# Value sums written straight into a value buffer, a fourth buffer for exponentials, and a new instruction order

## The chip, the cores and the metric

One Trainium2 chip, one of its cores. The metric is the device time of one execution, in microseconds (us). A kernel is run several times and the median is given beside the lowest and the highest. The profile comes from one further execution, in which every instruction's start and duration are recorded; its span is the time from the first to the last instruction, and a little more than the span passes before and after it.

## The reference

Two stages. The first is attention over 4 batches, 8 heads, 768 positions and 64 channels a head. Each position attends to its neighbours within a window of 16 and to 24 summaries, one for each block of 32 positions (the maximum of the block's keys, the mean of its values):

```
k_sum = k.reshape(B, H, nb, block, D).max(axis=3)
v_sum = v.reshape(B, H, nb, block, D).mean(axis=3)
scores_l = scale * q @ k.T, masked to |i - j| < 16
scores_s = scale * q @ k_sum.T + log(block)
a = softmax(concat(scores_l, scores_s));  out = a @ concat(v, v_sum)
```

The second stage takes the attention's output as x (4 x 768 x 512):

```
theta = x @ w_theta
y = w_tok_r @ (x * cos(theta)) + w_tok_i @ (x * sin(theta))
u = x + y
result = u + max(u @ w_ch, 0)
```

All of it has to be near float32; the four weight matrices arrive as 64-bit floats.

## The kernel before, in words

The work of a batch is cut into six tiles of 128 positions, 24 tiles in all. For a tile the kernel makes the scores (group S, line 522), subtracts and reduces them on DVE (L558), takes exponentials on ACT (L562), transposes these on PE (group PT, L571), copies the transposed exponentials out of PSUM (L577, on ACT or DVE), multiplies them by the values (group AV, L545), normalises (L586 to L595) and transposes the result (group X, L604). Then come theta (group TH, L638 for batch 0, L643 later), its sine and cosine (L654 to L667, ACT with DVE), the products with x (L673, DVE or POOL, called Z below) and the mixing over positions: groups M (L701, batches 0 and 1) and MP (L816, batches 2 and 3, seven products m = 1 to 7 in place of eight). The results stay in x or go to memory, and at the end groups CP (L921) multiply by w_ch and write out.

Before the first tile of a batch, `prepass` (L430) makes the summaries: maxima of keys with DVE reductions (L445), sums of values on PE (batch 0: L449, three loads `vn`, each for two matmuls) or DVE (batches 1 to 3: L465, four loads `vT`, then a transpose on PE, L469). ACT scales the value sums into a small tile `vs` (L472), a memset writes the ones beside them (L474), and `att_tile` copies `vs` into the first 24 rows of each of the four value buffers `v` of the batch (L494). The other rows of `v` are loaded (`vg`).

The weights are put together from 64-bit words by five elementwise steps (L400 to L411) on ACT, POOL and DVE, through a ring of three buffers `f`, which the loads `kT` and `vT` of later batches share. The exponentials and their transposed copies share a ring of EB = 3 buffers `e`: a tile needs two for its halves and two for the copies.

Every operation is recorded first, with the engines that may run it, and gets a number. Then the table `ORDER` (L54) gives the whole order: it lists the numbers, with a letter where the engine is not the default one (d for DVE, g for POOL). Each engine runs its own part strictly in this order, as does the DMA queue on SP, which issues all loads and stores. So an instruction that waits holds up all that stand behind it on its engine. The data dependences and the rings of buffers decide what an instruction waits for; the order decides what it stands behind.

Names used below: S0 is the score group of tile 0, PT5 the transposes of tile 5, M3 the mixing groups of tile 3 of batch 0 (two weights and two halves of the columns, so four groups), MP6 product 6. PSUM banks are called t, s0, s1, pa0, pa1, m0, m1 and m2.

Of the kernel before, what the change touches and what calls it, by code (L numbers as in the profile page):

```python
# [7 lines left out]
F32 = mybir.dt.float32  # L8
# [4 lines left out]
AF = mybir.ActivationFunctionType  # L13
# [4 lines left out]
B, H, S, D = 4, 8, 768, 64  # L18
P = 128
NT = S // P  # L20
NP = H // 2
# [33 lines left out]
27 31 0 23 11 8g 25 9 1g 17g 29 24 13 18 14 19 2 26 86 3 10 4 44 5 20 30 48 32 39 87 21 33 28 47g 6 45 49g 88 46 89 7 50 35  # L55
239g 79 51 185 52 42 190 40 60 100 62 64 34 36 55 238 66 56 191g 240 61 54 12 90 194 91 63 241g 192g 53 80d 59 93 15 58 193 92
67 57 37 65 195 81 68 38g 295g 69 82 83 196 70d 235 41 43g 84 186 71 200 101 188 199 197 187g 107 198 102g 108 203 290 72 76d
204 73 205 206 22 294 201 94 202 189g 77 85 74 207 208 95g 103 211 75d 242 78d 223 104 96 210 212 209 224 243 213 247 296g 97
245 214d 98 109 225 215 293g 244 237 105 249 118 216 119g 99 226 236 246 251 110 217 250 220 227 252 106 228 254 253 218 111
120 123 255 221 248 257 297 345 124g 258 121 219d 256 229 349g 291 222d 130 122 259 260 306 125 703g 262 230 261d 292 308 270  # L60
263 231 131g 351g 307 310 309 312 126 271 313 267 298 300 268 264 301 302 115 350g 112 348g 272 311 127 113 132 273 265 135
304 274 299 305 303 136g 266d 275 141 269d 133 142g 314 137 315 352 276 317 423 277 138 316 325 134 326 232 143 163 353 139
278 318 116 144 164g 233 424g 145 327 355 328 329 361 146 364 363 279 322d 330 422g 117 165 347 280 282 283 284 319d 331 365
281 323 166 320 168 354 332 346 321 324d 147g 419 337 362 359 169g 366 356 368 285 357 360 380 167 338 358 367 369 148 333 140
425 170 370 381 152 234 339 382 372 149 150 371 153 114 334 383 171 154 373 172 400 374 426 128 155 375 156 157 158g 335 384
376 129 385 401 340 377 159 174 435 378 402 386 379 392 387 175g 454 160 421 176 161 343 394 388 455 456 389 177 427 457 404
# [212 lines left out]
def attn_moe(tc, qg, kg, vg, kT, vT, vn, wth, wtr, wti, wch, out, tune=TUNE):  # L279
# [145 lines left out]
    f_th, f_t, w_th, w_t = [], [], [], {}  # L425


    ksum, vsum, keys, kbuf, vbuf = {}, {}, {}, {}, {}

    def prepass(b, due):  # L430
        pr.late, pr.key = K["R_PRE"], ("PRE", b * NT)
# [690 lines left out]
```

## Time and profile before

| | us |
|---|---|
| median of 3 runs | 437.54 |
| lowest, highest | 436.19, 440.58 |
| the profiled execution | 436.54 |
| its span | 434.8 |
| busy in it: PE, DVE, ACT, POOL | 422.1, 345.6, 295.2, 197.5 |

The profiled execution took 1.7 us more than its span. Busy time counts an instruction from its start to its end; matmuls overlap each other and their weight loads (PEld), so starts that follow each other tell more of PE than durations do. Idle time of an engine is put down to the instruction that ended it last.

### The profile page before, as it was taken

How to read it: one execution, taken by the hardware profiler on the slowest of the kernel's cores; microseconds unless marked ns; L12 is line 12 of the kernel's file. 1: busy time of each engine (PE TensorE's matmuls, PEld its weight loads, DVE VectorE, ACT ScalarE, POOL GpSimd, SP SyncE). 2: the span in 40 equal slices, each digit the busy share in tenths (PEclk: the TensorE clock that was granted, in tenths of full speed). 3: DMA queues.
4: the chain of work that ended last, by engine and by line, in shares of the span. 5: the costliest groups of instructions: out<-in, count | busy, mean ns of one | idle time of the engine just before them, and what ended most of it. 6: DMA issues, size and time to landing. Idle time of an engine off the chain costs nothing.

```text
span 434.8 us, 10046 instructions
## 1 busy us (share of the span) xinstructions
PE 422.1 (97%) x3682; PEld 351.0 (81%) x3682; DVE 345.6 (79%) x940; ACT 295.2 (68%) x624; POOL 197.5 (45%) x201
## 2 busy tenths in 40 slices
PE   6889999999999999999999999999999999999996
PEld 2455555667888888888878899899899899999996
DVE  3899999788777675678487678946489999899896
ACT  2899996897677878886677876876643465545310
POOL 2552315755647565254246854485332211344541
PEclk9999999999999999999999999999999999999999
DMA  8999878899774977787787877757468795401436
GB/s 301 361 361 351 317 230 284 249 283 286 225 278 140 244 219 210 229 242 212 249 231 200 269 242 228 228 171 210 139 205 313 252 335 174 158 19 56 145 133 231
DMA packets 76321, 100.07 MB, mean 230 GB/s; under 512 B 23024, under 2 KB 58864, under 8 KB 76272
## 3 DMA queue, kind: packets, MB, share of 16 engines
q1 hardware_dynamic: 76272, 99.43, 72.1%
q8 instruction: 29, 0.48, 0.4%
q14 instruction: 20, 0.16, 0.1%
HBM read 75.82 MB, written 23.59 MB: 229 GB/s over the span
## 4 chain that ended last, share of the span: by engine, by line
PE 80%; DMA 12%; DVE 3%; ACT 1%; SPq 1%; issue 1%; POOL 0%; DVEq 0%; POOLq 0%
PE m L701 21%; PE m L816 18%; PE t L643 10%; PE c L921 7%; PE m L921 6%; PE pa L545 5%; PE s L522 4%; DMA wt<-wtr 3%; PE t L638 3%; DMA f<-vT 3%; PE t L604 2%; PE pa L571 2%; DMA wth<-wth 2%; DMA v<-vg 2%; SPq L302 1%; PE t L921 1%
## 5 line engine op out<-in xcount | busy, mean ns | idle before, releaser
L816 PE MATMUL m<-wt,hl 128*128 128x384 f32 x504 | 96.1, 339 | 1.6 <-ACT hl L308 0.9
L816 PEld LDWEIGHTS m<-wt,hl 128*128 128x128 f32 x504 | 87.8, 188 | 5.1 <-ACT hl L308 1.6
L701 PE MATMUL m<-wt,hl 128*128 128x512 f32 (+1 forms) x432 | 85.0, 341 | 0.0
L701 PEld LDWEIGHTS m<-wt,hl 128*128 128x128 f32 x432 | 68.5, 188 | 10.9 <-issue 0.2
L562 ACT ACTIVATE e<-e,st 128x118 f32<-128x118 f32 x192 | 64.6, 388 | 10.7 <-DVE st L558 9.8
L558 DVE CUSTOM_DVE_ANT_0 e<-s,cs 128x118 f32<-128x118 f32 x192 | 46.2, 272 | 6.1 <-PE s L522 2.9
L643 PE MATMUL t<-wth,xh 128*128 128x512 f32 x144 | 45.6, 398 | 0.0
L317 POOL TENSOR_TENSOR hl<-zu,hl 128x512 fp32r<-128x512 f32 x22 | 29.7, 1353 | 20.5 <-DMA wt<-s_scratch 5.9
L673 POOL TENSOR_TENSOR zu<-xn,zu 128x512 f32<-128x512 f32 x22 | 30.1, 1372 | 18.6 <-ACT zu L667 11.6
L308 ACT CAST hl<-zu 128x512 fp32r<-128x512 f32 x34 | 21.0, 618 | 18.4 <-PE m L816 18.2
L729 POOL TENSOR_TENSOR f<-f 128x192 f32<-128x192 f32 x28 | 18.9, 674 | 32.3 <-DVE hl L317 9.7
L701 PE MATMUL m<-wt,zu 128*128 128x512 f32 (+1 forms) x96 | 33.3, 490 | 0.0
L545 PEld LDWEIGHTS pa<-v,e 118*64 118x64 f32 x768 | 24.9, 137 | 7.3 <-issue 2.0
L545 PE MATMUL pa<-v,e 118*64 118x65 f32 x768 | 28.2, 224 | 1.2 <-ACT e L577 0.9
L701 PEld LDWEIGHTS m<-wt,zu 128*128 128x128 f32 x96 | 17.7, 190 | 14.0 <-issue 12.7
L643 PE MATMUL t<-wth,xl 128*128 128x512 f32 x72 | 28.5, 396 | 0.0
L317 DVE TENSOR_TENSOR hl<-zu,hl 128x512 fp32r<-128x512 f32 x38 | 27.8, 738 | 0.6 <-ACT hl L308 0.5
L522 PE MATMUL s<-k,q 64*64 64x118 f32 x768 | 25.4, 267 | 1.8 <-ACT k L499 1.7
L656 DVE SCALAR_TENSOR_TENSOR zu<-zu,t 128x512 f32<-128x512 f32 x24 | 16.4, 683 | 12.6 <-ACT zu L654 12.6
L643 PEld LDWEIGHTS t<-wth,xh 128*128 128x128 f32 x144 | 24.0, 188 | 2.7 <-DVE st L587 0.2
L654 ACT ACTIVATE zu<-t,bmagic 128x512 f32<-128x512 f32 x24 | 16.4, 685 | 13.9 <-PE t L643 13.2
L522 PEld LDWEIGHTS s<-k,q 64*64 64x64 f32 x768 | 20.1, 132 | 7.1 <-ACT k L499 2.5
(185 smaller groups left out, 903.7 us busy)
## 6 DMA issues: line engine op xcount, KB each, us to landing
wt<-s_scratch SPq DMA_DIRECT2D x48, 384.0 KB, 4.6
v<-vg SPq DMA_DIRECT2D x48, 195.0 KB, 5.5
s_scratch<-f SPq DMA_DIRECT2D x24, 384.0 KB, 3.1
k<-kg SPq DMA_DIRECT2D x18, 376.0 KB, 5.6
q<-qg SPq DMA_DIRECT2D x24, 256.0 KB, 6.1
wt<-wtr SPq DMA_DIRECT2D x6, 768.0 KB, 12.5
wt<-wti SPq DMA_DIRECT2D x6, 768.0 KB, 12.0
f_scratch<-wt SPq DMA_DIRECT2D x6, 768.0 KB, 7.0
```

Of the source, the lines that this page charges most:

```text
L308: nc.scalar.copy(dst(), src())
L317: lambda e: V[e].tensor_tensor(dst(), src(), hi().bitcast(F32), op=ALU.subtract), reads, writes, due, port=BOTH)
L522: mm(0.79 * len(pairs) / NP, [lambda p=p, g=g, h=h: nc.tensor.matmul(sc[h].get()[ROW[g], p], q.get()[ROW[h], p, ROW[g]], k.get()[ROW[h], p ...
L545: mm(2 * 0.433 + scores[0] + (0.2 if scores[0] else 0.0), [lambda n=n, g=g, a=a: nc.tensor.matmul(xa[a].get()[ROW[g], n], turned[g].get()[ ...
L558: op({"DVE": 0.205}, lambda eng, n=n: nc.vector.tensor_tensor_reduce(e()[:, n], sc[n % 2].get()[:, 2 * a + n // 2], mask(m), -SCALE, 3.0e3 ...
L562: op({"ACT": 0.288}, lambda eng, n=n: nc.scalar.activation(e()[:, n], e()[:, n], AF.Exp, bias=st.get()[:, n:n + 1], scale=-1.0), [(st, n)] ...
L643: calls = [lambda t=t, xx=xx, k=k, c=c: nc.tensor.matmul(th.get(), xx.get()[:, c], w_th[c].get()[:, k], start=(c == 0 and t == 0), stop=(c ...
L673: op({"DVE": c_dve(DM, "two"), "POOL": c_pool(DM)}, lambda e, z=z, hc=hc: V[e].tensor_tensor(z(), xn[b, i].get().rearrange("p h d -> p (h ...
L701: nc.tensor.matmul(acc[th](), zz, w[:, TT[th]], start=(s == 0 and r == 0 and t == 0 and (th == 0 or c == 0)), stop=(s == NT - 1 and r == 1 ...
L729: lambda e: V[e].tensor_tensor(dst(), x(), y(), op=ALU.add if sign > 0 else ALU.subtract), reads, writes, due, port=BOTH)
L816: calls = [lambda ref=ref, tt=tt, z=z, s=s, j=j, t=t, x=x, k=k, bank=bank, first=first: nc.tensor.matmul(bank[j].get()[:, :HT], z.get()[:, ...
L921: calls = [lambda k=k, t=t, x=x, y=y: nc.tensor.matmul(to.get(), weights[n][x][0]()[:, k, j * P:(j + 1) * P], operands[n].get()[:, y, k], ...
```

## The change

Four things are changed.

- ACT writes the scaled value sums straight into the first value buffer of the batch, not into `vs`, and the ones go there too. The other three buffers are filled by copies from the first. That is one copy less in each batch, and the tile `vs` is gone. The four value buffers of a batch are now taken in `prepass`, not at its first tile.
- The value sums of batch 0 are accumulated in the bank m0, which the mixing uses from its first group on, no longer in pa0. For batches 1 to 3 the bank is the same as before.
- The ring of exponentials' buffers has four in place of three (EB=4).
- The table ORDER is another one: all instructions may stand elsewhere, and many elementwise ones run on another engine. Nothing else is computed.

```diff
 ORDER = """
-27 31 0 23 11 8g 25 9 1g 17g 29 24 13 18 14 19 2 26 86 3 10 4 44 5 20 30 48 32 39 87 21 33 28 47g 6 45 49g 88 46 89 7 50 35
...
-            A1=13, T1=10, PREP=5, ..., HL=4, EB=3, TAU_A=8.2, TAU_M=4,
+            A1=13, T1=10, PREP=5, ..., HL=4, EB=4, TAU_A=8.2, TAU_M=4,
...
         if b < K["VSPE"]:
-            pv = Ref(ps, [P, NP, P], tag="pa0")
+            pv = Ref(*((pm, [P, DM], F32, "m0") if b == 0 else (ps, [P, DM], F32, "pa0")))
...
-        vs = Ref(apool, [NB, H, DV], tag="vs")
+        vbuf[b] = [Ref(apool, [NB + VL, H, DV], tag="v", bufs=K["VB"]) for _ in range(K["VB"])]
+        first = vbuf[b][0]
         op({"ACT": c_act(DM, True)}, lambda e: nc.scalar.activation(
-            vs.get()[..., :D], pv.get()[:NB].rearrange("n p (h d) -> n (p h) d", d=D), AF.Copy, scale=1.0 / BLK), [pv], [(vs, "v")], due)
-        op({"POOL": 0.12, "DVE": 0.1}, lambda e: V[e].memset(vs.get()[..., D:], 1.0), [], [(vs, "one")], due, port=BOTH)
-        ksum[b], vsum[b] = ks, vs
+            first.get()[:NB, :, :D], totals(), AF.Copy, scale=1.0 / BLK), [pv], [(first, "sum")], due)
+        op({"POOL": 0.12, "DVE": 0.1}, lambda e: V[e].memset(first.get()[:NB, :, D:], 1.0), [], [(first, "sum")], due, port=BOTH)
+        ksum[b] = ks
...
-            if 2 * i + g < K["VB"]:
+            if 0 < 2 * i + g < K["VB"]:
                 op({"POOL": c_pool(H * DV, False), "ACT": c_act(H * DV), "DVE": c_dve(H * DV, "fast")}, lambda e, g=g: (
-                    nc.scalar.copy if e == "ACT" else V[e].tensor_copy)(v[g].get()[:NB], vs.get()), [vs], [(v[g], "sum")], due, port=BOTH)
+                    nc.scalar.copy if e == "ACT" else V[e].tensor_copy)(
+                    v[g].get()[:NB], vbuf[b][0].get()[:NB]), [(vbuf[b][0], "sum")], [(v[g], "sum")], due, port=BOTH)
```

The lines from 475 on stand three further down in the changed kernel: L558 becomes L561, L562 becomes L565, L577 becomes L580, and so on.

Where the new order moves instructions, at three places. The first is the start, on DVE: `cs` are constants, `ks` the key maxima, `zu` the loaded keys, `xl` a weight being put together, `e,st` the scores of tile 0. Before:

```order
L339 MEMSET cs 128x3x24
L339 MEMSET cs 128x128
L445 TENSOR_REDUCE ks<-zu 128x24
L362 MEMSET bmagic 128x1
L363 MEMSET bright 128x1
L445 TENSOR_REDUCE ks<-zu 128x24 x3
L339 MEMSET cs 64x15
L404 TENSOR_SCALAR xl<-xl 128x512
L406 TENSOR_SCALAR xl<-xl 128x512
L339 MEMSET cs 64x15
L558 ISA e,st<-s_140,cs 128x118
```

Changed:

```order
L339 MEMSET cs 128x3x24
L445 TENSOR_REDUCE ks<-zu 128x24 x4
L339 MEMSET cs 128x128
L368 MEMSET beps 128x1
L339 MEMSET cs 64x15
L561 ISA e,st<-s_140,cs 128x118
```

All four reductions stand together, and the two steps of the weight (L404, L406) no longer stand between them and the first scores; L404 now runs on POOL and L406 comes four scores later. ACT, which makes the key operand of the score groups, goes with this. Before:

```order
L499 COPY k<-ks 128x4x24
L499 COPY k<-zu 128x2x94
L400 ACTIVATE xl<-wth_105 128x512
L499 COPY k<-zu 128x2x94 x2
L499 COPY k<-ks 128x8x24
```

Changed:

```order
L502 COPY k<-ks 128x8x24
L502 COPY k<-zu 128x2x94 x5
L400 ACTIVATE xl<-wth_123 128x512
L502 COPY k<-zu 128x2x94
```

The larger copy, which needs all four reductions, is now the first, and four of the five behind it serve tile 0. On the DMA queue the four loads of keys are the first four transfers; before, one load of values was the second of them.

The second place is near the end of the mixing of batch 3, on PE: bank m0 with product 6 (the rows up to hl_4606 before, hl_4622 now) and then with product 7. Between the two, DVE has to read the bank (L825). Before:

```order
L816 MATMUL m2_4488<-wt_1607,hl_4567 128x384 x3
L816 MATMUL m2_4488<-wt_1721,hl_4606 128x384 x3
L816 MATMUL m2_4488<-wt_1799,hl_4606 128x384 x3
L816 MATMUL m0_4572<-wt_1607,hl_4567 128x384 x3
L816 MATMUL m0_4572<-wt_1721,hl_4606 128x384 x3
L816 MATMUL m0_4572<-wt_1799,hl_4606 128x384 x3
L816 MATMUL m0_4572<-wt_910,hl_4629 128x384 x3
L816 MATMUL m2_4488<-wt_910,hl_4629 128x384 x3
```

Changed:

```order
L819 MATMUL m0_4560<-wt_1576,hl_4622 128x384 x3
L819 MATMUL m0_4560<-wt_1844,hl_4622 128x384 x3
L819 MATMUL m2_4512<-wt_1576,hl_4622 128x384 x3
L819 MATMUL m2_4512<-wt_1844,hl_4622 128x384 x3
L819 MATMUL m0_4560<-wt_1077,hl_4613 128x384 x3
```

Before, product 7 follows product 6 in m0 at once; now two groups in m2 stand between them.

The third place is on ACT at tiles 16 to 19: the sines (L666, L667 before) need another table than the exponentials. Before:

```order
L666 ACT_TABLE_LOAD
L666 ACTIVATE zu<-zu,bright 128x512
L667 ACTIVATE zu<-zu 128x512
L577 COPY e<-pa_3364 118x512
L654 ACTIVATE zu<-t,bmagic 128x512
L494 COPY v<-vs 24x520
L586 ACTIVATE st<-pa_3434,beps 128x4
L586 ACTIVATE st<-pa_3443,beps 128x4
L660 ACTIVATE zu<-zu 128x512
L666 ACTIVATE zu<-zu,bright 128x512
L667 ACTIVATE zu<-zu 128x512
L562 ACT_TABLE_LOAD
```

Changed:

```order
L565 ACTIVATE e<-e,st 128x118 x2
L589 ACTIVATE st<-pa_3428,beps 128x4
L589 ACTIVATE st<-pa_3437,beps 128x4
L669 ACT_TABLE_LOAD
L669 ACTIVATE zu<-zu,bright 128x512
L670 ACTIVATE zu<-zu 128x512
L565 ACT_TABLE_LOAD
L565 ACTIVATE e<-e,st 128x118 x2
```

Before, the sines of two tiles share one visit to the other table; now the sines of tile 17 have a visit of their own, amid the exponentials of tile 19. Over the whole program the table loads go from 32 to 36.

## Rows read from the trace of the kernel before

**Rows 1.** The page: busy us (share of the span) xinstructions of each engine.

```profile
PE 422.1 (97%) x3682; PEld 351.0 (81%) x3682; DVE 345.6 (79%) x940; ACT 295.2 (68%) x624; POOL 197.5 (45%) x201
```

**Rows 2.** Windows: length, busy us (count) of PE, PEld, DVE, ACT, POOL; clock, DMA share, GB/s.

```profile
7.14:44.74 37.60, 33.24 (x405) 18.38 (x404) 35.90 (x124) 31.80 (x79) 14.55 (x27) 1.00 1.03 363
44.74:205.00 160.26, 160.18 (x1546) 122.00 (x1545) 124.40 (x401) 130.29 (x275) 82.41 (x82) 1.00 0.80 244
205.00:260.00 55.00, 54.30 (x552) 46.39 (x551) 37.82 (x115) 41.05 (x92) 28.70 (x28) 1.00 0.77 232
```

**Rows 3.** Timeline of PE, the first mixing: start, us, what, xcount [idle before <-releaser].

```profile
44.74 6.61 PE L701 MATMUL m<-wt,zu 128*128 128x512 f32 x20
```

**Rows 4.** Timeline of DVE from the start.

```profile
7.14 0.95 DVE L445 TENSOR_REDUCE ks<-zu 128x24 f32<-128x768 f32 x1 [5.99 <-DMA zu<-kT]
...
8.18 2.78 DVE L445 TENSOR_REDUCE ks<-zu 128x24 f32<-128x768 f32 x3
...
12.70 0.28 DVE L558 CUSTOM_DVE_ANT_0 e<-s,cs 128x118 f32<-128x118 f32 x1 [0.43 <-PE s L522]
...
43.54 0.69 DVE L673 TENSOR_TENSOR zu<-xn,zu 128x512 f32<-128x512 f32 x1
```

**Rows 5.** Timeline of SP's DMA issues from the start.

```profile
1.26 0.42 SPq L302 DMA_DIRECT2D x<-vn  x1
1.74 1.42 SPq L302 DMA_DIRECT2D zu<-kT  x3
```

**Rows 6.** Groups of DVE up to 44.3 us: xcount | busy us, mean ns | idle before.

```profile
L577 DVE COPY e<-pa 118x512 f32<-118x512 f32 x3 | 2.1, 687 | 0.2 <-ACT v L494 0.2
L595 DVE TENSOR_TENSOR xn<-pa,st 128x256 f32<-128x256 f32 x6 | 2.2, 416 | 0.0
L404 DVE TENSOR_SCALAR xh<-xh 128x512 f32<-128x512 f32 x1 | 0.4, 448 | 0.0
```

**Rows 7.** Timeline of ACT at the start.

```profile
11.01 0.59 ACT L499 COPY k<-zu 128x188 f32<-128x188 f32 x2
11.50 0.35 ACT L499 COPY k<-ks 128x192 f32<-128x192 f32 x1
```

**Rows 8.** Timeline of PE and DVE at the end of the mixing of batch 3.

```profile
345.98 6.51 PE L816 MATMUL m<-wt,hl 128*128 128x384 f32 x36 [0.86 <-ACT hl L308]
...
344.72 0.69 DVE L408 SCALAR_TENSOR_TENSOR zu<-wth,zu 128x512 int32<-128x512 int32 x1
345.32 0.55 DVE L825 TENSOR_TENSOR x<-m,x 128x384 f32<-128x384 f32 x1
```

**Rows 9.** Timeline of PE at tiles 16 and 17.

```profile
212.45 0.68 PE L571 MATMUL pa<-cs,e 64*118 64x64 f32 x16 [0.48 <-DVE xn L595]
...
226.38 0.68 PE L571 MATMUL pa<-cs,e 64*118 64x64 f32 x15 [0.23 <-ACT xn L593]
```

**Rows 10.** Timeline of PE: theta groups before a mixing and before a value group.

```profile
246.21 0.63 PE L643 MATMUL t<-wth,xh 128*128 128x512 f32 x2
...
246.91 0.69 PE L816 MATMUL m<-wt,hl 128*128 128x384 f32 x3
247.43 0.62 PE L643 MATMUL t<-wth,xh 128*128 128x512 f32 x2
...
248.22 1.15 PE L545 MATMUL pa<-v,e 118*64 118x65 f32 x32
```

**Rows 11.** Groups of ACT: the table loads ahead of the sines.

```profile
L666 ACT ACT_TABLE_LOAD x16 | 20.5, 1283 | 0.2
```

**Rows 12.** Timelines of PE, DVE and POOL at tile 4.

```profile
68.44 9.19 PE L701 MATMUL m<-wt,zu 128*128 128x512 f32 x28
...
71.40 0.68 DVE L656 SCALAR_TENSOR_TENSOR zu<-zu,t 128x512 f32<-128x512 f32 x1
72.00 1.99 DVE L465 TENSOR_REDUCE vt<-f 128x24 f32<-128x768 f32 x2
...
74.10 1.27 POOL L673 TENSOR_TENSOR zu<-xn,zu 128x512 f32<-128x512 f32 x1 [0.58 <-ACT zu L667]
```

More of the change, by code (lines that the diff above doesn't have):

```diff
@@ L59 @@
[L59 to L66, printed above, removed]
@@ new lines @@
+1214 1135 1129 888g 1276 1061d 1130 1277d 1070 1141 1161g 1062 1278g 1103d 1068 1092 1247 894g 1117 1234 1279 895 1143 1093
+889d 1105 1280 1140 1132 1106 891 1281 1107 1104 1133 1125 896g 1282 1118g 890 1094d 1108 1215 1109 897 1283 1095d 892 1244
+1096 1111 1097 1100d 1225 1115 898g 1113 1142 1155g 899 1098 1134 1171 1284 1099d 1119 1216 1120 1285 1101 1102d 1121 900
+1162g 1172 1286d 1227 1302 1174 1226 1157 1231 1303 1168 1304 1287 1305 1144 1145 1217 1158 1228 1156g 1180 1181 1306 901
+1146d 1122 1176 1173 1229 1175 1184 1307 1182 1183 1308 1147 1178 1148 1248 1159 1378 1149 1150 1187 1169 1185 1288g 1219g
@@ new lines @@
+1583 1266 1334 1367g 1267 1314g 1204 1200 1368 1324 1221 1338 1589 1268 912g 1326 1220 1333 1369 1269 1325 1385 1595 1273d
+1361 913g 1236 1222 1362 914 1584g 1270 1271 1337 1274 1370 1459 1328 1272 1330 915 1223 1371 1318 1394 1596g 1329 1327 1275d
+1398 1241 1372 1386 920 1335 1242 1387 1590g 1397 1373 1290 1336 1381 1395 1224 1388 1374 1413 1292 1396 1375 909 1339 1414d
+1607g 1340 1415d 1416 1462 921g 1243 1585 1293 1377 1380 916g 1417 1341 1342d 1418 1291 1298 1319 1391 1591 1419 1392 1677
@@ L425, in attn_moe @@
     f_th, f_t, w_th, w_t = [], [], [], {}
-    ksum, vsum, keys, kbuf, vbuf = {}, {}, {}, {}, {}
+    ksum, keys, kbuf, vbuf = {}, {}, {}, {}
     def prepass(b, due):
@@ L447, in prepass @@
         if b < K["VSPE"]:
-            pv = Ref(ps, [P, NP, P], tag="pa0")
+            pv = Ref(*((pm, [P, DM], F32, "m0") if b == 0 else (ps, [P, DM], F32, "pa0")))
+            totals = lambda: pv.get()[:NB].rearrange("n (h d) -> n h d", d=D)
             product = lambda t, st: lambda: nc.tensor.matmul(
-                pv.get()[:NB].rearrange("n p d -> n (p d)"), member(t), st(), start=(t == 0), stop=(t == NT - 1))
+                pv.get()[:NB], member(t), st(), start=(t == 0), stop=(t == NT - 1))
             if b == 0:
@@ L484, in att_tile @@
             kbuf[b] = []
-            vbuf[b] = [Ref(apool, [NB + VL, H, DV], tag="v", bufs=K["VB"]) for _ in range(K["VB"])]
         pr.late, pr.key = K["R_KV"], ("KV", b * NT + i)
-        x, ks, vs = xt[b], ksum[b], vsum[b]
+        x, ks = xt[b], ksum[b]
         q = Ref(apool, [P, NP, P], tag="q", bufs=K["QB"])
```

155 lines of the change are left out of this document (78 added, 77 removed).

## The prediction

> **What bounds the kernel now.** I read the page first, then the windows by stage, then timelines where PE waits, then groups for durations. The page shows PE busy for 422.1 of 434.8 us, so only 12.7 us of its span are idle [rows 1]. The windows tell where: in 7.14 to 44.74 us PE is idle for 37.60 - 33.24 = 4.4 us, in 44.74 to 205 for 0.1 us, in 205 to 260 for 0.7 us [rows 2]; the other 7.5 us lie before 7.14 and behind 260. From the first mixing on [rows 3] the kernel is bound by PE; the granted clock is 1.00 in all three windows, so nothing is to be won there. The change leaves PE's 3682 matmuls as they are, so it can win only in waits, and in how often one shape of matmul follows another.
>
> Before 44.74 us the bound is another. DVE idles 5.99 us for the first keys, and from then until the first mixing it is busy for 35.90 of 37.60 us; the product that the first mixing needs last is its own, from 43.54 to 44.23 [rows 2, 3, 4]. What DVE saves up to that product moves the first mixing, and with it all behind.
>
> **The change part by part.** The sum is made against the profiled execution, 436.54 us, which is 1.0 below the median of the runs shown and 0.35 above the lowest of them.
>
> *The copy and the tile `vs`.* One copy less for each batch, on ACT or POOL; the other three now follow a small tile in the first value buffer. In the first batch this stands beside a DVE that is full, later beside a PE that is full [rows 2]: 0. If that cover were gone, the one copy saved in a batch would be a fraction of a microsecond in 37.60; I leave it within the bounds of the next term.
>
> *The fourth exponentials' buffer and bank m0 for the sums of batch 0.* Each removes a wait. The buffer lets exponentials run further ahead of the value groups; in the stage that PE fills there is no wait to remove (0.1 us of 160.26). Bank m0 frees the transposes of tile 0 from the reading of pa0; what decides at the start is DVE, not PE. Both 0 by themselves; what they allow is in the order.
>
> *(a) The start.* Three things.
> First, the keys. In before one load of values is issued at 1.26, ahead of three of the four key loads [rows 5]. Now it is behind them. It is 128 x 2 x 512 floats, 0.52 MB, or 1.4 us at the 363 GB/s of this stage [rows 2]. If the transfers share the engines, the first reduction starts 1.4 us sooner than 7.14; if the first load, issued before both, is served alone, not at all.
> Second, DVE's work before the product at 43.54. By the order it loses three copies of transposed exponentials (3 x 0.69), one step L404 (0.45), half a normalisation (0.42) and a memset (0.1): 3.0 us. It gains two weight scalings (L996 before; two scalar operations of the size of L404, so 2 x 0.45), one L404 on 768 columns (0.45 x 768/512 = 0.67) and 0.2 of small steps: 1.8 us. Net 1.2 us less [rows 6].
> Third, a new hole. The four reductions now stand together and end at about 7.14 - 1.4 + 0.95 + 2.78 = 9.5. ACT's wide copy needs all four; then come five more, four for tile 0. In before these took 0.35 and 0.30 each, and from the end of the last (11.85) to the first scores on DVE (12.70) passed 0.85 [rows 4, 7]. So scores start at 9.5 + 0.35 + 5 x 0.30 + 0.85 = 12.2: hardly sooner than 12.70. DVE waits 2.7 us there with 0.2 of memsets to do, 2.5 idle; in before it had 1.74 between the last reduction and the scores, filled with two steps of some 0.5, so 0.7 idle. 1.8 us more idle, nearly what the first two win.
> Sum of (a): -1.4 - 1.2 + 1.8 = -0.8. One end: the hole is filled or hidden and even the 1.70 us that DVE was idle in the window [rows 2] go, -1.4 - 1.2 - 1.7 = -4.3. The other: the keys come no sooner, -1.2 + 1.8 = +0.6.
>
> *(b) Bank m0 in the last mixing.* Product 7 stood right behind product 6 in m0 and PE waited 0.86 us. The timeline names a load, but PE starts at 345.98 just after DVE's reading of the bank (345.32, 0.55 long) ends at 345.87, and that stood behind a weight step [rows 8]. Now two groups lie between, 6 matmuls of 6.51/36 = 0.18, 1.1 us: -0.9. What is late next could be that same reading, behind another step of 0.69: 0.86 + 0.69 - 1.1 leaves 0.4 of wait, so the range is -0.9 to +0.4.
>
> *(c) Tiles 16 and 17.* Transposes waited 0.48 and 0.23 us for normalised values [rows 9]. The new order puts other work around them; I take -0.4. Range -0.7 to +1.0 (a wait like that of (b) in their place).
>
> *(d) More changes of shape on PE.* From a theta group to a mixing group the step is 246.91 - 246.21 = 0.70; to a value group 248.22 - 247.43 = 0.79, so 0.09 more before small tiles [rows 10]. By the order of PE there are 37 entries from full-size groups into groups of small tiles, 30 before: 7 x 0.09 = +0.6, range 0 to +1.2.
>
> *(e) New tight places.* In the fifth tile, between its theta group and its first mixing group, seven mixing groups stood in before, 9.19 us [rows 12]; now four, 4 x 1.31 = 5.2 us. The chain between them: ACT's first step (about the 0.7 of DVE's), then from DVE's L656 at 71.40 to the end of POOL's product at 74.10 + 1.27 = 75.37 is 4.0 [rows 12], so 4.7. It fits by 0.5 us, but a reduction of about 1.0 (1.99 for two) now stands ahead of L656 on DVE: 0 to 1.5 us late. And ACT loads tables 36 times, not 32: 4 x 1.28 = 5.1 us of ACT [rows 11], some of them in 205 to 260, where ACT is idle for 55.00 - 41.05 = 14 us [rows 2]. Between 0 (all in those 14 us) and 5.1 (all on the way of PE) I take +0.5, near the nearest row, since in 44.74 to 205 ACT was busy 130.29 of 160.26 with some fifteen such loads and PE waited 0.1.
>
> The table loads on ACT have almost no idle time before them and 1283 ns each [rows 11]. The Trainium skill (ScalarE: Activation LUTs, section "What ACT_TABLE_LOAD costs") gives the same 1283 ns for the load but adds a drain of some 1380 ns, 2.66 us for a switch. By the page the four would take an estimated 10.6 us of ACT; by the rows they take 5.1, and no such drain stands there as idle time. The rule speaks against the change, and weighs less here than the rows.
>
> Sum: -0.8 - 0.9 - 0.4 + 0.6 + 0.5 = **-1.0**, so 435.5 against the profiled execution. A median lies up to 1.0 above such an execution; I forecast half of that, **436.0 us**, 1.5 below the median of before and within 1% of it (about what a measurement of this kernel can tell from no change).
>
> **Rivals.**
> *R1, the start is worth more (faster).* DVE's load alone decides when the first mixing starts, the hole is filled by scores that come in sooner, and M0 starts at 44.74 - 4.3 = 40.4. With (b), (c) and (d): -4.3 - 0.9 - 0.4 + 0.6 = -5.0, so 431.5. For it: DVE is busy for 95% of that window. Against it: 2.5 us of hole follow from the order itself, and after it ACT, busy for 31.80 of 37.60 [rows 2], must keep up.
> *R2, the extra table loads reach PE (slower).* In 205 to 260 the sines of tile 17 stand amid the exponentials of tile 19, so exponentials come up to 2 x 1.28 late for each separate visit. If ACT has nothing in hand there, the four loads reach PE whole: +5.1 + 0.6, with (b) and nothing from the start: +4.8, 441.3. It decides once PE's idle time in 205 to 300 exceeds the 0.7 of before by more than about 2.5 us. For it: the timeline already shows waits on ACT there [rows 9]. Against it: the 14 us of idle ACT and a fourth buffer that lets exponentials go ahead.
> *R3, the order does nothing.* PE was dense, the start is held by its key loads and copies, and gains and losses are below 0.5: 436.5 to 437.5.
>
> **How the numbers follow.** The main case 0.45 (432.5 to 439), R1 0.25, R2 0.18, R3 0.12. Faster by over 1% means below 433.2: R1 mostly and little of the main case, 0.26. Slower means above 441.9: the upper half of R2, and tight places of (e) and (c) at their ends together, 0.14. Within: 0.60. The range takes in most of R1, whose value is 431.5, and of R2 at 441.3: 430.3 to 441.5.
>
> **What would show it.** Right: the first reduction on DVE starts between 5.7 and 7.1, the first scores near 12.2 with about 2.5 us idle ahead, the first mixing near 44; no wait of PE on m0 near 345; at tile 4 less than 1.5 us of wait; idle time of PE in 205 to 260 near 1 us. Wrong: a first mixing at 41 or earlier (R1), or idle time of PE over 3 us in 205 to 300 that ends at exponentials (R2). The forecast is wrong altogether if PE's busy time differs by more than 2 us at the same 3682 matmuls, since I cost it at 0.6.

## The result and the profile after

| us | before | after |
|---|---|---|
| median of 22 runs each | 437.94 | 440.97 |
| lowest, highest | 436.19, 440.58 | 438.73, 445.28 |
| the profiled execution, its span | 436.54, 434.8 | 438.83, 437.1 |
| start of the first mixing | 44.74 | 45.28 |

The changed kernel is slower: its time is 1.0075 of before's, interval 1.0056 to 1.0094, or 3.3 us. The forecast was 436.0, 1.5 faster; the range (430.3 to 441.5) holds the median, the sign is wrong. The profiled execution after is 2.3 us longer than that of before. It is also a lucky one: it lies 2.1 us below its kernel's median, that of before 1.4 below.

The page after, the line of all engines, answers to [rows 1]:

```profile
PE 424.9 (97%) x3682; PEld 351.7 (80%) x3682; DVE 346.5 (79%) x940; ACT 292.7 (67%) x620; POOL 202.9 (46%) x202
```

PE is idle for 437.1 - 424.9 = 12.2 us, less than the 12.7 before, and the span is longer. Busy time isn't work: the 3682 matmuls are the same, and PE is "busy" 2.8 us longer. The windows after answer to [rows 2] (length, busy us and count of PE, PEld, DVE, ACT, POOL, then clock, DMA share, GB/s):

```profile
7.14:44.74 37.60, 32.77 (x390) 17.51 (x390) 32.52 (x123) 32.12 (x80) 16.53 (x29) 1.00 1.04 354
44.74:205.00 160.26, 160.19 (x1530) 121.57 (x1526) 126.43 (x388) 120.64 (x265) 87.31 (x83) 1.00 0.80 241
205.00:260.00 55.00, 55.00 (x618) 46.42 (x612) 40.25 (x141) 44.31 (x91) 30.71 (x29) 1.00 0.82 250
```

In the first stretch DVE is busy for 32.5 us, 3.4 less than before, so the load that was to go has gone, and more. But PE reaches the first mixing later. From 44.74 to 205 both kernels show a full PE, yet after has 1530 matmuls there and before 1546: no idle time, and fewer matmuls begun (the count depends also on which shapes fall into the window). In 205 to 260 the 0.7 us of idle time are gone.

At the start, DVE's timeline after (start, us, what, idle before and its releaser) answers to [rows 4]:

```profile
5.14 1.81 DVE L445 TENSOR_REDUCE ks<-zu 128x24 f32<-128x768 f32 x2 [4.12 <-DMA zu<-kT]
7.36 1.81 DVE L445 TENSOR_REDUCE ks<-zu 128x24 f32<-128x768 f32 x2 [0.41 <-DMA zu<-kT]
...
12.16 0.28 DVE L561 CUSTOM_DVE_ANT_0 e<-s,cs 128x118 f32<-128x118 f32 x1 [1.63 <-POOL k L502]
```

The keys come 2.0 us sooner (5.14, before 7.14), the first scores at 12.16 (12.70), with the hole ahead of them that the order showed. SP's issues and PE's timeline of the same execution say what else moved (they answer to [rows 5] and [rows 3]):

```profile
0.82 1.82 SPq L302 DMA_DIRECT2D zu<-kT  x4
2.68 0.43 SPq L302 DMA_DIRECT2D x<-vn  x1
```

```profile
9.13 1.88 PE L450 MATMUL m<-x,vt 128*24 128x512 f32 x4 [1.21 <-DMA x<-vn]
...
16.44 1.04 PE L525 MATMUL s<-k,q 64*64 64x118 f32 x32 [0.48 <-DMA q<-qg]
...
23.93 1.24 PE L548 MATMUL pa<-v,e 118*64 118x65 f32 x32 [0.92 <-ACT e L565]
...
31.67 0.66 PE L607 MATMUL t<-cs,xn 128*128 128x128 f32 x4 [1.09 <-DVE zu L659]
...
43.24 1.02 PE L641 MATMUL t<-xl,x 128*128 128x512 f32 x2
44.19 1.15 PE L548 MATMUL pa<-v,e 118*64 118x65 f32 x32
45.28 7.15 PE L704 MATMUL m<-wt,zu 128*128 128x512 f32 x21
```

The load of values is issued at 2.68 in place of 1.26. PE's value sums wait for it, and on PE the scores of tile 0 stand behind them. From 43.24 on PE goes from theta to a value group to the mixing without a gap: here PE itself is the bound, not DVE. Before does the same, one value group earlier (PE's timeline of before):

```profile
31.83 0.66 PE L604 MATMUL t<-cs,xn 128*128 128x128 f32 x4 [1.16 <-DVE zu L656]
...
40.12 1.15 PE L545 MATMUL pa<-v,e 118*64 118x65 f32 x32
41.20 1.12 PE L638 MATMUL t<-xh,x 128*128 128x512 f32 x2
...
43.88 1.02 PE L638 MATMUL t<-xl,x 128*128 128x512 f32 x2
```

At the transposes near 31.7 both kernels have done the same matmuls, and after is 0.2 us ahead. From there to the first mixing, with the same matmuls to do, it takes 13.6 us where before takes 12.9. So in this profile the start is lost behind 31.7 us, and not at its first loads.

At tiles 16 and 17 the waits of [rows 9] are gone. Both transposes follow at once:

```profile
214.67 0.68 PE L574 MATMUL pa<-cs,e 64*118 64x64 f32 x16
...
228.79 0.68 PE L574 MATMUL pa<-cs,e 64*118 64x64 f32 x16
```

At the end of the mixing of batch 3, PE's timeline answers to [rows 8], with DVE's of the same time behind it:

```profile
341.09 7.00 PE L819 MATMUL m<-wt,hl 128*128 128x384 f32 x39 [0.75 <-ACT zu L400]
348.46 6.35 PE L819 MATMUL m<-wt,hl 128*128 128x384 f32 x33 [0.37 <-DMA wt<-s_scratch]
355.04 3.21 PE L819 MATMUL m<-wt,hl 128*128 128x384 f32 x17 [0.22 <-DVE x L828]
```

```profile
338.50 0.43 DVE L404 TENSOR_SCALAR zu<-zu 128x512 f32<-128x512 f32 x1 [0.68 <-ACT zu L400]
338.84 0.68 DVE L732 TENSOR_TENSOR zu<-zu 128x512 f32<-128x512 f32 x1
339.44 0.42 DVE L406 TENSOR_SCALAR zu<-zu 128x512 int32<-128x512 int32 x1
339.77 1.68 DVE L828 TENSOR_TENSOR x<-m,x 128x384 f32<-128x384 f32 x3
```

The wait between products 6 and 7 is gone. In its place PE waits 0.75 ahead of product 6, while DVE's readings of the banks (L828) stand behind steps on the channel weights, the first of which waited for ACT; and 0.37 for weights ahead of the second group of product 7.

The table loads of ACT, which answer to [rows 11], cost what they did, and no idle time of PE in 205 to 260 points at them:

```profile
L669 ACT ACT_TABLE_LOAD x18 | 23.1, 1283 | 0.2
```

To see what idle time doesn't show, take the stretch from the first mixing to the last matmul. It begins behind the same 410 matmuls in both kernels and holds the same 3272. Its windows, of before and of after (the counts take in matmuls that still run at the edge):

```profile
44.74:431.37 386.63, 384.16 (x3273) 330.80 (x3271) 308.79 (x814) 262.09 (x545) 179.76 (x162) 1.00 0.70 218
```

```profile
45.28:433.00 387.72, 386.22 (x3276) 331.32 (x3272) 310.90 (x813) 258.79 (x540) 183.94 (x162) 1.00 0.70 216
```

PE's idle time falls from 2.5 to 1.5 us, and still the stretch is 1.1 us longer, because PE is busy 2.1 us longer with the same matmuls at the same clock. So the 2.3 us of the two profiled executions lie as follows: 0.5 until the first mixing; 1.1 from there to the last matmul (2.1 more busy, 1.0 less idle); and 0.7 from the last matmul to the end of the last store (4.1, before 3.5). What the 2.1 us are stands under (d) below. Some expectations go by another count, the usual distance between neighbouring groups on PE; it put 0.9 us on changes of neighbours and the small delays on waits. No view shows that count, and the results are read here without it.

### The profile page after: what moved, and what is told of

It reads as the page before. It is cut to its first block, busy times and chain, and to the rows that moved or that the text cites. A ratio compares the mean times of both kernels' runs of the same rounds, so it can differ in the third digit from the quotient of the medians.

```text
span 437.1 us, 10050 instructions
## 1 busy us (share of the span) xinstructions
PE 424.9 (97%) x3682; PEld 351.7 (80%) x3682; DVE 346.5 (79%) x940; ACT 292.7 (67%) x620; POOL 202.9 (46%) x202
## 4 chain that ended last, share of the span: by engine, by line
PE 86%; DMA 9%; ACT 1%; DVE 1%; SPq 1%; issue 0%
PE m L704 25%; PE m L819 16%; PE t L646 12%; PE c L924 7%; PE m L924 6%; PE pa L548 5%; PE s L525 4%; PE t L641 4%; PE pa L574 3%; DMA v<-vg 3%; PE t L607 2%; DMA wth<-wth 2%; DMA wth<-wch 2%; DMA x<-vn 1%; DMA wt<-s_scratch 1%; PE t L924 1%
## 5 line engine op out<-in xcount | busy, mean ns | idle before, releaser
L704 PE MATMUL m<-wt,hl 128*128 128x512 f32 (+1 forms) x432 | 87.8, 344 | 0.0
L565 ACT ACTIVATE e<-e,st 128x118 f32<-128x118 f32 x192 | 64.1, 389 | 2.8 <-DVE st L561 2.2
L561 DVE CUSTOM_DVE_ANT_0 e<-s,cs 128x118 f32<-128x118 f32 x192 | 45.0, 272 | 12.6 <-ACT xn L596 6.1
L732 POOL TENSOR_TENSOR f<-f 128x192 f32<-128x192 f32 x28 | 20.3, 724 | 37.3 <-DMA f<-f_scratch 14.6
L676 POOL TENSOR_TENSOR zu<-xn,zu 128x512 f32<-128x512 f32 x21 | 28.2, 1343 | 19.7 <-ACT zu L670 9.6
L317 POOL TENSOR_TENSOR hl<-zu,hl 128x512 fp32r<-128x512 f32 x20 | 26.5, 1329 | 14.8 <-DVE zu L732 4.8
L548 PEld LDWEIGHTS pa<-v,e 118*64 118x64 f32 x768 | 24.9, 137 | 9.2 <-issue 3.0
L317 DVE TENSOR_TENSOR hl<-zu,hl 128x512 fp32r<-128x512 f32 x40 | 30.0, 753 | 1.4 <-ACT hl L308 1.4
L525 PE MATMUL s<-k,q 64*64 64x118 f32 x768 | 24.9, 267 | 0.5 <-DMA q<-qg 0.5
```

The costliest lines, as they stand in the source:

```text
L317: lambda e: V[e].tensor_tensor(dst(), src(), hi().bitcast(F32), op=ALU.subtract), reads, writes, due, port=BOTH)
L525: mm(0.79 * len(pairs) / NP, [lambda p=p, g=g, h=h: nc.tensor.matmul(sc[h].get()[ROW[g], p], q.get()[ROW[h], p, ROW[g]], k.get()[ROW[h], p ...
L548: mm(2 * 0.433 + scores[0] + (0.2 if scores[0] else 0.0), [lambda n=n, g=g, a=a: nc.tensor.matmul(xa[a].get()[ROW[g], n], turned[g].get()[ ...
L561: op({"DVE": 0.205}, lambda eng, n=n: nc.vector.tensor_tensor_reduce(e()[:, n], sc[n % 2].get()[:, 2 * a + n // 2], mask(m), -SCALE, 3.0e3 ...
L565: op({"ACT": 0.288}, lambda eng, n=n: nc.scalar.activation(e()[:, n], e()[:, n], AF.Exp, bias=st.get()[:, n:n + 1], scale=-1.0), [(st, n)] ...
L676: op({"DVE": c_dve(DM, "two"), "POOL": c_pool(DM)}, lambda e, z=z, hc=hc: V[e].tensor_tensor(z(), xn[b, i].get().rearrange("p h d -> p (h ...
```

## The experiments

Nearly all kernels have the code of one kernel and an order that is put together from the two: the operations of one order up to a point, the rest in the order of the other. Ratios are to before, with runs of before on the same chip. The start is that until the first mixing.

**Code or order.** The code of after, the order of before:

```diff
 code: after (EB=4, sums into the value buffer, bank m0)
-ORDER of after
+ORDER of before, without the four copies
```

> The code of after (no copy of the sums, bank m0, four exponentials' buffers) with the order of before. If the code itself costs (value sums now hold a value buffer and bank m0), this is slower than before by some 3 us, near 441; if the order alone costs, it is the time of before, 437.9 within 0.8, and its span is near 434.8 with the first mixing at 44.7.

Measured: 438.23, ratio 1.0018 (0.9998 to 1.0037). The code costs at most 0.4% and may cost nothing; the slower time comes with the order. The new order in turn needs the fourth buffer for exponentials, so it couldn't be tried with three.

**The start or what is behind it.** Two kernels, joined at the first mixing:

```diff
 code: after
-ORDER of after
+first run: ORDER of before until the first mixing, then of after
+second run: ORDER of after until the first mixing, then of before
```

> The code of after, the order of before up to the first mixing, and the order of after from there. If the start is what loses (first mixing at 45.28 in place of 44.74), this gains 0.5 us or more on after: 440.3 or less, and 438 if the start were the whole loss. If the loss lies behind the first mixing (PE's order of shapes, +0.9 by its starts, and the end), it stays within 0.6 of after, 440.4 to 441.

> The code of after, the order of after up to the first mixing, and the order of before from there. If the start is the whole loss: 441. If it costs what the first mixing shows: 438.4, first mixing at 45.3. If what lies behind decides: 438 to 438.5.

Measured: 441.19 with the old start (1.0087, 1.0054 to 1.0119) and 440.82 with the new one (1.0081, 1.0050 to 1.0112). Both are as slow as after, so neither half carries the loss alone. And the joint itself costs. With the old start, value group 4 waits for a copy of DVE, which comes out of the old start 0.8 us later than out of the new one (PE's timeline):

```profile
58.76 1.22 PE L548 MATMUL pa<-v,e 118*64 118x65 f32 x32 [1.11 <-DVE e L580]
```

With the new start a transpose waited 1.68 us at 96.76. So both runs overstate what they were to measure. Their profiles tell more than their times: from the first mixing on PE is busy for 386.1 us with the new order there, and for 384.7 with the old one.

**The end.**

```diff
 code: after
-ORDER of after
+ORDER of before until 326 us (first groups of batch 3's mixing), then of after
```

> The code of after, the order of before up to the first groups of the mixing of batch 3 (326 us), and the order of after from there. If the end loses (from there PE's waits and neighbours give some +0.4, the last stores +0.65 in one profile): 438.5 to 439. If the end loses nothing: 437.9 within 0.4. If the whole loss is there: 441.

Measured: 439.79, ratio 1.0063 (1.0043 to 1.0083), against 1.0018 with the whole old order. The new end costs 0.45%, about 2 us, with an uncertainty of some 1.2. This joint costs too: its profile has a wait of 0.61 at 329.23, ahead of a mixing group, that neither kernel has. How much of the 2 us is the end's own stays open.

**DVE's queue ahead of product 6.** Two tries on after; the second also moves the step that waits for ACT.

```diff
 DVE near 338 us
-L404, L732, L406, L828 (MA2), L828 (MA1, bank of product 6), L828 (MA1)
+first: L828 (MA2), L404, L732, L828 (MA1), L406, L828 (MA1)
+second: L828 (MA2), L732, L828 (MA1), L404, L406, L828 (MA1)
```

> After, with two of DVE's readings of the mixing's banks (L828) put ahead of steps on the channel weights near 338 us. If the wait of 0.9 us ahead of product 6 comes from that queue on DVE, it falls to 0.2 or less, the first group of product 7 comes 0.6 to 0.9 earlier, and the time is 440.2 where after has 441. If it comes from the loads of the channel weights on ACT, as the timeline's releaser says, the wait stays near 0.9 and the time at 441.

> After, with DVE's two readings near 338 us ahead of both steps on the channel weights, the one that waits for ACT included. If the reading that stood behind a step waiting for a load is the cause of the 0.9 us ahead of product 6, that wait is 0.2 or less now (it was 0.7 with the second step alone moved), and the span from there to the end is 0.6 to 0.9 shorter. If ACT's casts are the cause it stays at 0.7 or more.

Measured: 1.0068 (1.0041 to 1.0095) and 1.0072 (1.0046 to 1.0098), no better than after. In the second the first group of product 6 waits no more. PE's timeline of that run:

```profile
342.04 6.54 PE L819 MATMUL m<-wt,hl 128*128 128x384 f32 x36 [0.71 <-DVE x L828]
348.96 6.23 PE L819 MATMUL m<-wt,hl 128*128 128x384 f32 x33 [0.39 <-DMA wt<-s_scratch]
```

The wait is still 0.71, one group later: the group in the other bank waits for the other reading, behind the two steps that were moved. So it was DVE's queue, and not the step of ACT that the profile of after names; and taking it from one group hands it to the next. The expected 0.6 to 0.9 didn't come.

The profile of the first try is worth a look for another reason. At 24.86 its PE had waited 1.35 us, and the next matmuls ran at half speed (PE's timeline, then two windows):

```profile
24.86 1.70 PE L548 MATMUL pa<-v,e 118*64 118x65 f32 x32 [1.35 <-POOL k L502]
26.50 2.08 PE L641 MATMUL t<-xh,x 128*128 128x512 f32 x2
```

```profile
20.00:25.00 5.00, 3.60 (x85) 2.96 (x83) 4.67 (x30) 4.88 (x14) 3.52 (x7) 1.00 1.04 309
25.00:30.00 5.00, 5.00 (x52) 2.99 (x55) 3.90 (x12) 3.82 (x11) 2.22 (x3) 0.66 1.04 364
```

The pair took 2.08 us where after's profile has 1.13, the granted clock is 0.66 in that window (part of it at 1.2 GHz, part at 2.4), and the first mixing came at 47.3 with an order that gave 45.3 in the profile of after. The edit lies 300 us behind; so much can the same start differ from one execution to another.

**PE's neighbours.** Five groups of after moved by 2 to 4 places in 60 to 110 us, which saves 1.0 us by the count of usual steps:

```diff
 PE (mixing group, scores, value group, scores, value group)
-M4 between AV5 and S7; S5 before PT4; AV4 amid TH3; S10 behind TH7; AV7 between X6 and M5
+M4 behind PT6; S5 behind PT4; AV4 ahead of TH3's last two; S10 behind X7; AV7 ahead of X6
```

> After, with five groups of PE moved by 2 to 4 places between 60 and 110 us, so that small tiles follow small tiles more often: by the steps measured in the traces 1.0 us less. If PE's neighbours are a part of the loss, the last matmul ends about 1.0 earlier than in after (432.0 where after has 433.0) and the time is 440. If waits take their place, or the steps don't add up, there is no difference: 441.

Measured: 448.58, ratio 1.0222 (1.0180 to 1.0264). New waits of up to 1.8 us came at several places between 57 and 119 us, for example 1.83 ahead of the scores of tile 10 and 0.99 ahead of a value group for its copy; behind the first mixing PE idles for 7.5 us, in after for 1.5. So the run doesn't show whether the steps add up; the other profiles do, under (d) below. What it shows is how little slack the order has: five groups moved by a few places brought 6 us of waits.

**Product 7 alone.** The change's way at [rows 8], in the kernel before:

```diff
 PE, mixing of batch 3
-MP6, m0: MP7 of tile 18, m2: MP7 of tile 18, m0: tile 19, m2: tile 19
+MP6, m2: MP7 of tile 18, m2: tile 19, m0: tile 18, m0: tile 19
```

> Before, with two groups of product 7 in bank m2 put ahead of its first in m0 (what the change does there, alone). If the bank decides, the wait of 1.03 at 344.4 falls to 0.2 or less and the time is 436.6 where before has 437.5. If the loads of product 7's weights are just behind it, a wait of 0.5 stands at its second or third group and the gain is 0.5 or less.

Measured: 438.04, ratio 0.9994 (0.9969 to 1.0018), no difference. PE's timeline there:

```profile
335.76 13.99 PE L816 MATMUL m<-wt,hl 128*128 128x384 f32 x76
350.04 2.38 PE L816 MATMUL m<-wt,hl 128*128 128x384 f32 x12 [0.29 <-DMA wt<-s_scratch]
353.31 1.31 PE L816 MATMUL m<-wt,hl 128*128 128x384 f32 x6 [0.89 <-DMA wt<-s_scratch]
```

PE runs through from product 6 to product 7, so the bank was the cause of the 0.86 of [rows 8] (the 1.03 at 344.4 of the expectation is no idle time of the timeline). Then it waits 0.29 and 0.89 for weights. These are loaded into the place of product 6's, so a load can be issued only when product 6 has passed: in after SP issues six of them from 342.40 on, each as a pair of groups of product 6 ends (342.37, 343.41, ...), and the load for tile 19 lands some 5 us later, at 348.4. A PE that comes sooner meets its loads. The next limit stood right behind the bank's wait, and removing that wait alone gives nothing.

**The order of the first loads.** Once in after, once in before:

```diff
 SP, first loads
-after: kT kT kT kT vn q wth ...
+in after: kT vn kT kT kT wth q ... (as before)
-before: kT vn kT kT kT wth q ...
+in before: kT kT kT kT vn q wth ... (as after)
```

> After, with the loads of the first 45 us in the order of before (a load of values second, ahead of three of the four key loads). If the start hangs on the keys and DVE, the first mixing comes 1 us or more later than in after (46.3 or later). If it doesn't, the reductions start 1 to 2 us later and the first mixing stays within 0.4 of 45.3; the time then is 441 within 0.8.

> Before, with the loads of the first 45 us in the order of after (all keys ahead of the first values). If the keys decide the start, as the prediction had it, the first mixing comes up to 1.4 us earlier than in before, near 43.5 to 44.5, and the time is 436 to 437. If the loads as a whole bind, the first value sums and what stands behind them on PE come later by about as much, the first mixing is at 44.7 or later and the time 437.4 or more.

Measured: after with the old loads 1.0103 (1.0072 to 1.0134), first mixing at 47.4; before with the keys first 439.45, ratio 1.0038 (1.0021 to 1.0055), first mixing at 46.9. The second is the cleanest result of all: one change of the load order, 1.7 us lost (0.9 to 2.4). Its DVE and PE at the start:

```profile
5.26 0.95 DVE L445 TENSOR_REDUCE ks<-zu 128x24 f32<-128x768 f32 x1 [4.10 <-DMA zu<-kT]
...
14.94 0.28 DVE L558 CUSTOM_DVE_ANT_0 e<-s,cs 128x118 f32<-128x118 f32 x1 [1.98 <-PE s L522]
```

```profile
9.38 3.46 PE L449 MATMUL pa<-x,vt 128*24 128x512 f32 x4 [2.47 <-DMA x<-vn]
12.77 1.13 PE L378 MATMUL t<-zu 128*128 128x512 f32 x2
13.83 1.04 PE L522 MATMUL s<-k,q 64*64 64x118 f32 x32
```

The keys are there 1.9 us sooner, and the first scores reach DVE 2.2 us later. PE waits 2.47 us for values, and then the sums take 3.46 us in place of the 1.88 that the same four matmuls take in after's profile. The windows of the first 20 us give a granted clock of 0.91. In the run of after with the old loads, PE waited 2.21 for key copies instead, with the same 0.91. Each order of loads fits the order of PE and ACT that it was made with.

**The wait or the clock.** The kernel of the last run, and after, with more of the idle matmuls that PE already has at its start (they compute nothing that is used):

```diff
 PE at the start
-in before with keys first: idle x3, PRE, idle, S0
+idle x5, PRE, idle, S0
-in after: idle x4, PRE, S0
+idle x5, PRE, S0
```

> Before with all keys loaded first (as e13), and with PE's idle matmuls ahead of and behind the first value sums: one moved there, two added, which compute nothing. If PE's clock is what makes that start slow, it is 1.00 in the first 20 us (0.91 in e13), the first value sums take 1.9 in place of 3.5, the first mixing comes at 45.5 or earlier (46.9) and the time is 438 or less. If it is the loads alone, the first mixing stays near 46.9 and the time near 439.5.

> After with one more idle matmul of PE ahead of the first value sums, where PE waits 1.2 to 2.3 us for their load. If the clock's fall in the start makes after's slow executions (6 of 22 at a mean clock below 0.9975, 2.9 us slower), they become rare and the median falls to 440 or less. If not, it stays at 441 and as many are slow.

Measured in before with keys first: 438.22, ratio 1.0019 (0.9992 to 1.0046), where it was 1.0038 without them. The windows of the first 20 us, without and with the added matmuls, and PE's sums with them:

```profile
0.00:20.00 20.00, 15.08 (x96) 5.41 (x98) 9.77 (x36) 7.76 (x22) 5.94 (x22) 0.91 0.93 330
```

```profile
0.00:20.00 20.00, 16.29 (x104) 6.61 (x104) 10.67 (x39) 8.80 (x24) 6.62 (x23) 1.00 0.93 321
```

```profile
9.72 1.88 PE L449 MATMUL pa<-x,vt 128*24 128x512 f32 x4 [0.47 <-DMA x<-vn]
```

The values land as late as before, PE's clock stays whole, and the sums take 1.88. Over all its executions the mean granted clock lies below 0.9975 in 1 of 12, against 8 of 12 without the fillers. (Both added matmuls stand ahead of the sums; behind them there is one, as there was.) So the clock's fall behind the wait looks like a good part of that loss; the two intervals still overlap. One part of the expectation failed: in its profile the first mixing comes at 48.3, for other waits (for example 1.19 ahead of the transposes at 34.07 and 0.82 for a load at 43.70), and that execution, 439.62, was one of the slower ones of its kernel. In after the filler did nothing good: 442.23, ratio 1.0107 (1.0066 to 1.0149), with 2 of 6 executions below 0.9975. There PE's clock was whole until 20 us already; in the two profiles with the same start that show a fall, it comes near 25 and 35 us.

The clock doesn't make after the slower kernel, though. Of its 22 executions 6 have a mean granted clock below 0.9975; the other 16 have a median of 440.23. Of the 96 executions of before that were timed beside the runs of this section, 16 are below; the other 80 have a median of 437.4. At a whole clock the difference is still 2.8 us.

**Scores first.** After, with the first scores ahead of the value sums:

```diff
 PE: -PRE, S0, S0   +S0, S0, PRE
 ACT: -copy for tile 1, copies for tile 0   +copies for tile 0, copy for tile 1
```

> After, with the scores of tile 0 ahead of the first value sums on PE, and ACT's wide copy for tile 1 behind the copies for tile 0. If the start of after loses because the first scores stand behind sums whose load of values was moved behind the keys, the scores on DVE start near 10.7 in place of 12.16 and the first mixing comes at 44.5 or earlier, where four profiles of the start of after have 45.3 to 48.0 (mean 46.6); the time is 439.5 or less. If the loads of the whole first 25 us bind (values, queries), the scores come sooner and the first mixing stays at 45.3 or later; the time is 440.5 to 441.5.

Measured: 443.60, ratio 1.0117 (1.0087 to 1.0147), first mixing at 47.6. The scores then wait 2.87 for their queries, whose load stands behind the values; again the granted clock is 0.91 in the first 20 us. Of the rival expectation the late mixing holds, but the scores reach DVE at 12.64, later than the 12.16 of after, and the time is above its 441.5. That the loads bind there (354 GB/s in after's first window, 363 in [rows 2]) and that what one group wins the next one waits for fits this run; the fall of the clock has a part in it that the run doesn't separate.

**The stretch of tiles 16 and 17.** The order of before with that of after in between:

```diff
 code: after
-ORDER of after
+ORDER of before until 203 us, of after until 249, of before
```

> The code of after with the order of before, but the order of after between 203 and 249 us. PE's waits in 205 to 235 are 1.1 to 2.0 in five profiles of the order of before and 0.5 to 0.9 in those of after: 0.9 less expected there, 0.2 more for PE's neighbours. The time should be 437.5, 0.7 less than with the whole order of before (438.2), and might be the best of all. If the waits come back later in the same stretch, 438.2.

Measured: 452.28, ratio 1.0338 (1.0313 to 1.0363). Waits of 2.3 and 4.3 us at its second joint (the second ends with DVE's reading of a bank) hide what it was made for. Inconclusive.

**The middle.** Four more kernels cut the new order differently:

```diff
 code: after
+run 1: before until the first mixing, after behind it; three weight steps moved behind the late copy
+run 2: the same, and before again from 326 us on
+run 3: before until 78 us, after until 326, before
+run 4: before until 197 us, after until 326, before
```

> The code of after, the order of before up to the first mixing and that of after behind it, with three steps on weights moved behind the copy that the value group of tile 4 waited for in the first try (1.2 us). If the start is most of the loss: 438.5 or less. If the new order behind it loses 1.4, as the sum of PE's steps and waits over the profiles gives: 439 to 439.5. If it is all there: 440.5 or more.

> As the run before, and with the order of before from 326 us on: start and end old, the middle new. If PE's neighbours (+0.9 and some small steps) outweigh the waits saved at tiles 16 and 17 (-0.9): 438.3 to 439. If the middle is free: 437.5 to 438.2. If the end is free: as the run before.

> The code of after; the order of before until 78 us, of after from there to 326, of before behind it. By the steps of PE and the waits in the profiles the middle costs 1.0 for the neighbours, 0.5 for small steps in 100 to 205, gives 0.9 back at tiles 16 and 17: 438.8 where the whole order of before has 438.2. If the middle is most of the loss: 440 or more.

> The same with the order of before until 197 us. Neighbours +0.6, waits at tiles 16 and 17 -0.9: 437.9, no slower than the whole order of before (438.2). If the second half of the middle loses: 439 or more.

Measured: 1.0084 (1.0052 to 1.0115), 1.0086 (1.0058 to 1.0114), 1.0051 (1.0033 to 1.0069) and 1.0042 (1.0029 to 1.0054). In the first two the repair of the joint made another wait: a mixing group waits 1.03 us for a product on POOL (at 63.53 in the first, 63.66 in the second), and the second has another 0.92 ahead of scores at 82.67, so they overstate the loss by 1 to 2 us. The last two have clean joints but for 0.68 at 79.8 in the third. Against 1.0018 for the whole old order, the new middle costs 0.33% from 78 us on (some 1.4 us) and 0.24% from 197 us on (1.0 us), each with an uncertainty of about 1.1. The sums of steps and waits in the expectations were +0.6 and -0.3, so the second came out with the other sign, though 1.0 with that uncertainty may still be nothing. In its profile PE is busy 385.7 us behind the first mixing, 384.1 in that of the whole old order.

## Why the prediction was wrong

Two terms failed. (a) had the wrong sign, because DVE was taken for the bound of the start. (d) was priced at 0.6 us and measured 2.1 in the two profiles, because it priced only half of what a visit to small tiles costs; this is most of the loss.

*What bounds the start.* "What DVE saves up to that product moves the first mixing" is the step that failed. DVE was saved 3.4 us and the first mixing came 0.5 later. The row of 35.90 busy of 37.60 us [rows 2] was read as a bound, but it says only that DVE had work. Before's own timeline shows it: PE runs without a wait from the value group at 40.12 to the mixing at 44.74, and DVE's product had ended at 44.23, half a microsecond before.

*(a) -0.8.* Of its three parts, the first reduction came 2.0 sooner (1.4 expected), the scores at 12.16 (12.2 expected), and the hole was there: right in the rows, wrong in what follows. The term counted the load of values only as an obstacle to the keys. That PE's first group needs it, and that the scores stand behind that group on PE, wasn't followed up, nor what a waiting PE does to its clock. In the profile after (a) was +0.5; over the profiles with this start the first mixing lies at 45.3, 45.8, 47.3, 48.0 and 45.2 (mean 46.3), over ten with the start of before at 44.3 to 46.2 (mean 44.9). How much of the 3.3 us belongs to the start isn't settled: by these means 1.4, by the times between nothing and 2. The load order alone, in before, costs 1.7.

*(b) -0.9.* The wait went, as said, and the loads of weights and DVE's queue took its place: alone it gave 0.9994, and in after PE idles for 1.4 us in 325 to 362, in before for 1.6. The text asked "what is late next" and looked only at the same reading of the bank.

*(c) -0.4.* Right in sign: the 0.7 us of idle time in 205 to 260 are gone, the far end of its range. What that is worth in time no run shows by itself.

*(d) +0.6, range 0 to +1.2.* Right in kind and much too small. The prediction's own sign of being wrong was a difference of more than 2 us in PE's busy time; it is 2.8, of which 2.1 lie behind the first mixing. It isn't the chance of one profile. In the orders of the profiles, count the visits behind the first mixing: the times when PE goes from full-size groups to groups of small tiles (scores, transposes of exponentials, value groups). Profiles whose clock fell in that stretch are left out.

| visits | profiles | PE busy from the first mixing on, us |
|---|---|---|
| 28 (before) | 7 | 383.5 to 384.7 |
| 35 (new order from 197 to 326 us) | 1 | 385.7 |
| 39 (after) | 10 | 386.1 to 387.5 |

What a visit costs can be read where mixing groups of six stand among theta groups and among small tiles (PE's timeline after):

```profile
210.71 1.04 PE L525 MATMUL s<-k,q 64*64 64x118 f32 x32
211.68 1.31 PE L704 MATMUL m<-wt,hl 128*128 128x512 f32 x6
212.83 0.63 PE L646 MATMUL t<-wth,xh 128*128 128x512 f32 x2
...
213.53 1.21 PE L704 MATMUL m<-wt,hl 128*128 128x512 f32 x6
214.67 0.68 PE L574 MATMUL pa<-cs,e 64*118 64x64 f32 x16
...
220.63 1.20 PE L704 MATMUL m<-wt,hl 128*128 128x512 f32 x6
221.67 0.63 PE L646 MATMUL t<-wth,xh 128*128 128x512 f32 x2
```

From its start to that of the next group such a group takes 1.04 us between theta groups (at 220.63), 1.14 ahead of small tiles (213.53) and 1.15 behind them (211.68). The prediction priced the way in, at 0.09, and not the way back, 0.11. It also left out visits that come from the transposes X: the 30 entries of before are 37 with these, and in after they are 49. Eleven more visits behind the first mixing, at 0.10 and 0.11 each, are 2.3 us, an estimate from these rows, and the profiles show about as much. No run changes the visits alone: the one that moved PE's neighbours takes four away, and its new waits hide what that gave.

*(e) +0.5.* The chain at tile 4 was in time (PE idles 0.1 us from the first mixing to 100 us in both kernels), and nothing shows that the table loads reach PE. (In before 20 of them fall in 44.74 to 205 us, not some fifteen.) R2 gave a time close to the measured one, 441.3, by a mechanism that isn't there: ACT's loads cost 1283 ns each with 0.2 us idle in sum, and PE has no idle time in 205 to 260. R1 fell with the bound that it shared with the forecast.

*Not in the sum.* The time from the last matmul to the end of the last store (0.7 longer in the first two profiles; 3.9 to 4.3 us in ten profiles with the end of after, 3.5 to 3.9 in ten with that of before), and waits that differ from one execution to the next. The profiled execution was taken for the kernel, but after's lies 2.1 us below its median.

That (b), (c) and (e), -0.8 together, come close to the 1.0 us by which PE's idle time fell behind the first mixing is luck: most of it is (c)'s, (b)'s wait was replaced by others, and (e)'s loss wasn't there. With five terms of less than 1 us, each with its sign in doubt, a forecast of "faster" had no ground. The loss has no single place: the visits give some 2 us of it, and what the start and the end give isn't settled.

## What to carry to other kernels

An engine's busy share doesn't make it the bound; follow the last step before the stage that matters back on every engine, and ask of a load that is moved back which group waits for it and what stands behind that group. When a wait is removed from a pipeline that is dense, find the next two limits before counting the gain: here a bank, the loads of weights and a queue on DVE lay close behind each other. An engine without idle time can still take longer for the same work: compare the time that it takes for a stretch of equal work, count how often its instructions change their shape, and price the way back as well as the way in. In an order that is fixed by a list, an edit far from a gap is not neutral: of 18 orders and variants tried here, 15 were slower than before by more than their uncertainty, and none was faster.

## What was not expected of the hardware

A wait of PE near the start can cost more than its length. After 2.47 us without work the four matmuls of the value sums took 3.46 us in place of 1.88, at a granted clock of 0.91 over the first 20 us; in other runs waits of 2.87 and 2.21 us went with the same 0.91, and one of 1.35 at 24.9 us with 0.66 in the next 5 us. Matmuls that compute nothing went with a clock of 1.00 through the same late load. The Trainium skill (TensorE: Matmul & The Clock Gate, section "Part 1: The HAM clock gate (the "warmup" mystery)") describes such a fall of an idle engine's clock to half; the 2.08 us for a pair that takes 1.13 agree with it. Not every wait did this: 1.21 us in after, and 2.09 at the same place in the run of after with the filler, left the clock at 1.00 in the first 20 us.
